# A three-stage float32 kernel on one Trainium2 core: another product order in a phase's last block column, and steps moved to other places of the order

## The chip, the cores and the metric

The program runs on one core of one Trainium2 chip. The metric is the device time of one execution in microseconds (us); the time of a kernel is the median of its runs. A profiled execution gives, beside its own time, the start and the length of every instruction on each engine. PE is TensorE (matmuls), PEld its weight loads, DVE is VectorE, ACT is ScalarE, POOL is GpSimd, and SP is the engine whose queue issues all DMAs of this kernel.

## The reference

Three layers follow one another. B = 2 batches, 768 steps, 8 heads of 64; N = 1536 tokens, 512 features; 8 experts of width 1024; a dense layer of width 2048 whose weights come as 64-bit floats.

```python
def _attn_ref(q, k, v):          # decayed linear attention
    for t in range(S):
        state = gamma * state + einsum('bhd,bhe->bhde', k[:, :, t], v[:, :, t])
        y[:, :, t] = scale * einsum('bhd,bhde->bhe', q[:, :, t], state)

def _moe_ref(x, w_gate, w1, w2):
    logits = x @ w_gate
    P = exp(logits - logits.max())
    for _ in range(8):           # the gate iterations
        P /= P.sum(1, keepdims=True) + 1e-09
        P /= P.sum(0, keepdims=True) + 1e-09
        P *= N / E
    for e in range(E):
        out += P[:, e:e+1] * (maximum(x @ w1[e], 0.0) @ w2[e])

def _moe2_ref(x, w_in, w_out, alpha):
    h = x @ w_in
    g = maximum(h, 0.0) + alpha * minimum(h, 0.0)
    return g @ w_out
```

## The kernel before

After the attention (to 47 us) the kernel runs 20 **phases**, each one a pair of layers for one batch of 768 tokens: phases 0 to 7 are the experts for batch 0, phases 8 to 15 (FAST) the experts for batch 1, phases 16 to 19 the dense layer, cut into two halves of its width for each batch. Every float32 factor is held as two float32r pieces, a high half (a rounded copy, made by ACT) and a low half (the rest, made by DVE or POOL), and `mm3` makes three matmuls of each product of pieces.

**Layer 1** of a phase is computed as a Strassen-like scheme of 7 products for each of 4 block columns j, so 28 products of 6 matmuls. Product p of column j is called (j, p). The list `order` says in which order they stand, and a place in it is a position 0 to 27. What `after` does once a product is issued: (j,1) fills bank A, and ACT copies it to bank B; (j,5) fills D, which is copied to `d` in SBUF (ACT, in dense phases DVE); (j,6) adds to B, and DVE writes E = B + d; (j,7) adds to B again, which must wait until E has been made, and DVE makes B + d a second time (into D, in FAST phases into an SBUF tile `b22`); (j,4) adds to B once more, which must wait for that; (j,3) adds to E and (j,2) to A. `block` then turns a finished bank into the high and low halves of the next layer's input, with later steps of it kept in the list `late` and issued after the next product.

**Layer 2** of the phases outside FAST makes 6 token tiles; each is two half tiles of 12 matmuls over four of the eight blocks of the width ("t0a" uses columns 0 and 1, "t0" columns 2 and 3). These 12 half tiles are positions 28 to 39. FAST phases have a second Strassen-like scheme of 28 units u there, positions 28 to 55.

All other work is put by hand beside this order: `step(ph, pos, fn)` and `at(ph, key, fn)` hang a step behind the product or half tile at that position, and `do` issues the product, what `after` adds, and then the steps in the order in which they were registered. Every engine, SP too, works off its own instructions in the order in which they were issued, and a waiting one holds up those behind it. The steps that matter here:

- `w1_at`: layer 1's weights of column m (n is the phase's first column): four sums (`w1_sum`), then a high and a low half of three parts a, c and b. The low half of b is followed by `w_load(0, m + 2)`, the load of the column after the next into the same one of two buffers; before that buffer can be filled, the store of a part of it to `c1` (in `w1_high`) must have been read out.
- `w2_high`, `w2_low`: high and low halves of layer 2's weights v; the second low half is followed by `w_load(1, n + 2)`.
- `decode_at(ph, bits, power, join, store)`: a 512 KB tile `rd` of 64-bit weights is turned into float32: `bits` (three DVE operations, L702, L704, L707), `power` (ACT, L712), `join` (DVE, L718, L721), `store` (SP) and at once the load of the next tile into the same buffer (L692). A FAST phase decodes two tiles, the first at positions 5, 7, 8 and 10, the second at 19, 21, 23 and 25.
- `gate_max`, `shift`, `rows`, `cols`: the gate. `shift` has one small matmul (`mx`) whose bank DVE clears first (`zeroed`), then operations on DVE and ACT; each `cols` one small matmul (`cs`).
- In FAST phases `t1` to `t4`, `hhigh` and `hlow` (L903) prepare layer 2's input from `b11`, `b12`, `b21` and `b22`.

Of the kernel before, what the change touches and what calls it, by code (L numbers as in the profile page):

```python
# [16 lines left out]
B, H, S, D = 2, 8, 768, 64  # L17
# [28 lines left out]
def tile_kernel(ctx, tc, qkT, kv, ctab, w_gate, w1, w2, w_in, w_out, alpha, out):  # L46
# [254 lines left out]
    with tc.manual_schedule():  # L301
# [491 lines left out]
        def after(ph, n, j, p):  # L793
# [26 lines left out]
            elif p == 7:  # L820
                nc.vector.tensor_tensor(out=banks[n, "D"], in0=banks[n, "B"], in1=banks[n, "d"], op=add)  # L821
                block(ph, n, j, 1, 1, banks[n, "D"])
            elif p == 4:
                block(ph, n, j, 1, 0, banks[n, "B"])
            elif p == 2:
                block(ph, n, j, 0, 0, banks[n, "A"])
            elif p == 3:
                block(ph, n, j, 0, 1, banks[n, "E"])
# [185 lines left out]
        for j in range(1, NJ):  # L1014
            order += [(j, 1), (j, 5), (j - 1, 4), (j, 6), (j - 1, 3), (j, 2), (j, 7)]
        order += [(NJ - 1, 3), (NJ - 1, 4)]
        slots = [f"t{t}{w}" for t in range(TT) for w in ("a", "")]
        todo = []
# [3 lines left out]
        def step(ph, pos, *fns):  # L1022
            if pos >= 60:
                ph, pos = ph + 1, pos - 60
            for fn in fns:
                key = order[pos] if pos < 28 else pos - 28 if ph in FAST else slots[pos - 28]
                at(ph, key, fn)
# [27 lines left out]
        for ph in range(len(PHASES)):  # L1055
# [8 lines left out]
            elif ph < E:  # L1064
                decode_at(ph, 30, 31, 32, 33)
                decode_at(ph, 36, 37, 38, 39)
                prep_at(ph, dve, 9, 19, 9, 21, 23, 24, 27)
# [8 lines left out]
            if fast:  # L1076
# [3 lines left out]
                w1_at(ph, n + 5, pool, dve, 44, 44, 45, 48, 49, 50, 52)  # L1080
            else:
                if ph:
                    w1_at(ph, n + 2, pool, pool, 0, 3, 3, 6, 6, 9, 9)
                else:
                    w1_at(ph, n + 2, pool, pool, 0, 5, 5, 9, 9, 11, 11)
                if ph:
                    w1_at(ph, n + 3, pool, pool, 5, 10, 10, 12, 12, 16, 16)
                else:
                    w1_at(ph, n + 3, pool, pool, 10, 13, 13, 14, 14, 17, 17)
# [3 lines left out]
                early = ((4, 6, 7, dve), (9, 12, 13, dve), (15, 16, 20, dve), (22, 25, 26, dve))  # L1093
                usual = ((12, 12, 12, pool), (17, 17, 17, pool), (19, 19, 19, pool), (23, 23, 23, pool))
                first = ((6, 6, 7, dve), (12, 13, 14, dve), (18, 18, 18, pool), (23, 23, 23, pool))
                for j, (hi, l0, l1, eng) in enumerate(first if ph == 0 else early if ph < E else usual):
                    step(ph, hi, lambda m=n + j: w2_high(m))
                    step(ph, l0, lambda m=n + j, eng=eng: w2_low(m, 0, eng))
                    step(ph, l1, lambda m=n + j, eng=eng: w2_low(m, 1, eng))
# [3 lines left out]
            if fast:  # L1103
                decode_at(ph, 5, 7, 8, 10)
                decode_at(ph, 19, 21, 23, 25)
# [58 lines left out]
        at(0, (3, 4), lambda: sums.update(ps=zeroed("mx", 128)))  # L1164
        at(0, "t0a", shift)
        for it, key in enumerate(("t0", "t1a", "t1", "t2a", "t3a", "t3", "t4a", "t5a")):
            at(0, key, lambda it=it: cols(it))
        for m, keys in ((4, ("t0", "t1a", "t1", "t2a", "t2")), (5, ("t2", "t3a", "t3", "t4", "t4"))):
            at(0, keys[0], *(lambda m=m, q=q: w1_sum(m, q, dve) for q in (0, 1)))
            at(0, keys[1], *(lambda m=m, q=q: w1_sum(m, q, dve) for q in (2, 3)))  # L1170
            for part, key in zip("acb", keys[2:]):
                at(0, key, lambda m=m, part=part: w1_part(m, part, dve))
# [14 lines left out]
        for ph in range(len(PHASES)):  # L1187
# [12 lines left out]
            for t in range(TT):  # L1200
                do(ph, f"t{t}a")
                do(ph, f"t{t}")
# [77 lines left out]
```

## Time and profile before

| | us |
|---|---|
| runs, median (lowest to highest of 3) | 1285.27 (1284.57 to 1286.77) |
| the profiled execution, its time | 1281.88 |
| its span, first to last instruction | 1279.8 |
| PE busy | 1270.3 (99%) |
| DVE, ACT, POOL busy | 956.2 (75%), 639.8 (50%), 427.8 (33%) |
| granted TensorE clock, mean | 1.000 |

The profiled execution lies 3.4 us below the median of the runs, and 2.1 us of its time lie outside its span. Layer 1 of a phase takes some 29.5 us, layer 2 some 32.7 us (29.15 us in FAST phases). Matmuls are pipelined and their shown lengths overlap, so a busy PE still loses time where two starts lie further apart than usual: back to back, matmuls of 384 columns start 0.173 us apart, those of 512 columns 0.226 us.

### The profile page before, as it was taken

The numbers are of one execution on the slowest core, as the hardware profiler recorded it, in microseconds if no ns is written. First come the engines' busy times: TensorE is split into PE (matmuls) and PEld (weight loads), VectorE is DVE, ScalarE is ACT, GpSimd is POOL, SyncE is SP. The second block draws the span as 40 slices with busy tenths as digits, with TensorE's granted clock in tenths as the row PEclk, the third lists the DMA queues.
The fourth block names the chain that finished last, engine by engine and source line by source line (L and its number), as shares of the span: only waits on it lengthen the run. The fifth ranks groups of instructions, "written<-read, shape, count | busy, mean of one in ns | idle before, by whom it ended". The sixth has DMA issues, their size and how long they took to land.

```text
span 1279.8 us, 19739 instructions
## 1 busy us (share of the span) xinstructions
PE 1270.3 (99%) x7276; PEld 1180.6 (92%) x7276; DVE 956.2 (75%) x1551; ACT 639.8 (50%) x1157; POOL 427.8 (33%) x396
## 2 busy tenths in 40 slices
PE   9999999999999999999999999999999999999998
PEld 7888898989898989899999999999999998989897
DVE  6666888888888888868697887878797865686271
ACT  5643544444443435555545464646455473737270
POOL 5743252526161607000031402131304181616160
PEclk9999999999999999999999999999999999999999
DMA  9673898999999999877686858686775862242111
GB/s 357 213 232 120 264 338 277 320 291 312 300 311 291 316 306 306 283 259 239 236 264 217 291 190 289 197 276 206 269 228 190 310 216 83 83 140 93 48 34 50
DMA packets 150671, 295.76 MB, mean 231 GB/s; under 512 B 11904, under 2 KB 75440, under 8 KB 150576
## 3 DMA queue, kind: packets, MB, share of 16 engines
q1 hardware_dynamic: 150576, 294.52, 69.7%
q8 instruction: 57, 0.93, 0.3%
q14 instruction: 38, 0.31, 0.1%
HBM read 197.19 MB, written 97.28 MB: 230 GB/s over the span
## 4 chain that ended last, share of the span: by engine, by line
PE 88%; DVE 5%; ACT 2%; POOL 2%; issue 2%; DMA 1%; POOLq 0%; ACTq 0%
PE o L197 10%; PE o L199 10%; PE o L198 10%; PE B L197 8%; PE B L199 8%; PE B L198 8%; PE A L199 5%; PE A L198 5%; PE A L197 5%; PE D L199 3%; PE D L197 3%; PE D L198 3%; PE E L199 2%; PE E L198 2%; PE E L197 2%
## 5 line engine op out<-in xcount | busy, mean ns | idle before, releaser
L107 POOL TENSOR_TENSOR raw<-raw 128x256 f32<-128x256 f32 x112 | 100.6, 908 | 96.4 <-DMA raw<-wd 28.3
L179 POOL TENSOR_TENSOR pr<-pr 128x256 f32<-128x256 f32 x52 | 49.5, 952 | 205.3 <-DMA pr<-in_w_dram 202.2
L893 ACT ACTIVATE hs<-b 128x768 fp32r<-128x768 f32 x112 | 93.8, 845 | 32.7 <-PE A L199 11.4
L903 DVE TENSOR_TENSOR hs<-b,hs 128x768 fp32r<-128x768 f32 x96 | 92.8, 974 | 12.3 <-ACT hs L893 12.2
L935 POOL TENSOR_TENSOR total<-total,t 128x384 f32<-128x384 f32 x56 | 66.3, 1211 | 103.0 <-DVE t L931 102.7
L805 ACT ACTIVATE B<-A 128x384 f32<-128x384 f32 x80 | 38.7, 484 | 107.8 <-PE A L199 104.6
L808 DVE TENSOR_TENSOR E<-B,d 128x384 f32<-128x384 f32 x80 | 45.0, 562 | 61.7 <-PE B L199 56.8
L261 POOL TENSOR_TENSOR xs<-b,xs 128x384 fp32r<-128x384 f32 x6 | 8.8, 1464 | 197.7 <-ACT xs L257 197.7
L199 PE MATMUL B<-hs,ws 128*128 128x384 f32 x192 | 64.2, 334 | 0.0
L197 PE MATMUL B<-hs,ws 128*128 128x384 f32 x192 | 64.1, 334 | 0.0
L198 PE MATMUL B<-hs,ws 128*128 128x384 f32 x192 | 64.1, 334 | 0.0
L712 ACT ACTIVATE ex<-ex,ebias 128x512 uint32<-128x512 uint32 x32 | 23.0, 720 | 76.7 <-DVE ex L702 76.7
L183 ACT ACTIVATE pw<-pr 128x1024 fp32r<-128x1024 f32 x32 | 33.8, 1057 | 52.8 <-POOL pr L179 29.7
L857 DVE SCALAR_TENSOR_TENSOR total<-o,P,total 128x512 f32<-128x512 f32 x42 | 31.4, 747 | 37.1 <-PE o L199 36.9
L187 DVE TENSOR_TENSOR pr<-pr,pw 128x512 fp32r<-128x512 f32 x64 | 52.0, 843 | 0.0
L179 DVE TENSOR_TENSOR pr<-pr 128x256 f32<-128x256 f32 x76 | 46.9, 617 | 1.7
L851 ACT ACTIVATE total<-o 128x512 f32<-128x512 f32 x18 | 10.8, 598 | 68.1 <-PE o L199 68.1
L197 PE MATMUL A<-hs,ws 128*128 128x384 f32 x128 | 42.9, 335 | 0.0
L198 PE MATMUL A<-hs,ws 128*128 128x384 f32 x128 | 42.8, 335 | 0.0
L199 PE MATMUL A<-hs,ws 128*128 128x384 f32 x128 | 42.8, 334 | 0.0
L821 DVE TENSOR_TENSOR D<-B,d 128x384 f32<-128x384 f32 x48 | 26.8, 558 | 20.2 <-PE B L199 20.2
L800 ACT ACTIVATE d<-D 128x384 f32<-128x384 f32 x64 | 31.2, 488 | 15.9 <-PE D L199 15.8
(3441 smaller groups left out, 4656.8 us busy)
## 6 DMA issues: line engine op xcount, KB each, us to landing
ws<-c SPq DMA_DIRECT2D x112, 512.0 KB, 5.2
raw<-in_w_dram SPq DMA_DIRECT2D x64, 512.0 KB, 4.5
c<-raw SPq DMA_DIRECT2D x32, 512.0 KB, 5.9
pr<-in_w_dram SPq DMA_DIRECT2D x32, 512.0 KB, 5.9
c<-pw SPq DMA_DIRECT2D x32, 512.0 KB, 7.0
c<-pr SPq DMA_DIRECT2D x32, 512.0 KB, 7.2
raw<-c SPq DMA_DIRECT2D x32, 512.0 KB, 5.9
raw<-wd SPq DMA_DIRECT2D x32, 512.0 KB, 3.7
```

What stands on the lines that cost most here:

```text
L107: eng.tensor_tensor(out=out, in0=in0, in1=in1, op=op)
L179: eng.tensor_tensor(out=out, in0=in0, in1=in1, op=op)
L183: nc.scalar.activation(out=ph2[i], in_=pr[i], func=AF.Copy)
L187: nc.vector.tensor_tensor(out=pr[i][:, a].bitcast(F32R), in0=pr[i][:, a], in1=ph2[i][:, a].bitcast(F32), op=ALU.subtract)
L197: nc.tensor.matmul(ps, ah, bh, start=first, stop=False, skip_group_check=True)
L198: nc.tensor.matmul(ps, ah, bl, start=False, stop=False, skip_group_check=True)
L199: nc.tensor.matmul(ps, alo, bh, start=False, stop=last, skip_group_check=True)
L805: nc.scalar.activation(out=banks[n, "B"], in_=banks[n, "A"], func=AF.Copy)
L808: nc.vector.tensor_tensor(out=banks[n, "E"], in0=banks[n, "B"], in1=banks[n, "d"], op=add)
L893: nc.scalar.activation(out=t[:, 0, :], in_=hsource(ph, k), func=func)
L903: nc.vector.tensor_tensor(out=lo, in0=src, in1=hi.bitcast(F32), op=ALU.subtract)
L935: nc.gpsimd.tensor_tensor(out=dst, in0=dst, in1=tt[m, h], op=ALU.add)
```

## The change

It touches only the order in which work is issued and, at some places, the engine that does it.

- In the last column (j = 3) the order (3,1) (3,5) (2,4) (3,6) (2,3) (3,2) (3,7) (3,3) (3,4) becomes (3,1) (3,5) (3,6) (2,4) (2,3) (3,7) (3,2) (3,3) (3,4).
- Outside FAST, `block` of product 7 is no longer issued at once, but after the next product's own step.
- The second decoding of a FAST phase goes from positions 19, 21, 23, 25 to 15, 17, 20, 22.
- Phases 1 to 7: three low halves one position later.
- Dense phases: layer 2 begins with t0a, t1a, t0, t1; the weights v0 and v1 are split at position 1 (phase 16: 8 to 17) and v2's low half at 19.
- Phase 15: the sums of column 65 on DVE at position 42 instead of on POOL at 44.
- Phase 0: low halves of columns 2 and 3 partly on DVE; v1's low halves at 17 and 18 instead of 13 and 14; v2 and v3 at 20 and 24; columns 4 and 5 spread from position 22 on; the clearing of `mx` behind (3,3) and `shift` behind (3,4) instead of (3,4) and t0a, and the eight `cols` from t0a instead of t0.

```diff
--- before.py
+++ after.py
@@ -819,7 +819,7 @@
                     nc.scalar.activation(out=dst, in_=banks[n, key], func=AF.Relu)
             elif p == 7:
                 nc.vector.tensor_tensor(out=banks[n, "D"], in0=banks[n, "B"], in1=banks[n, "d"], op=add)
-                block(ph, n, j, 1, 1, banks[n, "D"])
+                late.append([lambda: block(ph, n, j, 1, 1, banks[n, "D"])])
             elif p == 4:
                 block(ph, n, j, 1, 0, banks[n, "B"])
             elif p == 2:
@@ -1011,10 +1011,17 @@
 
         pool, dve = nc.gpsimd, nc.vector
         order = [(0, 1), (0, 5), (0, 6), (0, 2), (0, 7)]
-        for j in range(1, NJ):
+        for j in range(1, NJ - 1):
             order += [(j, 1), (j, 5), (j - 1, 4), (j, 6), (j - 1, 3), (j, 2), (j, 7)]
+        j = NJ - 1
+        order += [(j, 1), (j, 5), (j, 6), (j - 1, 4), (j - 1, 3), (j, 7), (j, 2)]
         order += [(NJ - 1, 3), (NJ - 1, 4)]
         slots = [f"t{t}{w}" for t in range(TT) for w in ("a", "")]
+        paired = ["t0a", "t1a", "t0", "t1"] + slots[4:]
+
+        def slots_of(ph):
+            return paired if ph >= 2 * E else slots
+
         todo = []
         for ee in range(2):
             todo += [(k, NJ * ee + j, half) for k in range(2) for j in range(NJ) for half in range(2)]
@@ -1023,7 +1030,7 @@
             if pos >= 60:
                 ph, pos = ph + 1, pos - 60
             for fn in fns:
-                key = order[pos] if pos < 28 else pos - 28 if ph in FAST else slots[pos - 28]
+                key = order[pos] if pos < 28 else pos - 28 if ph in FAST else slots_of(ph)[pos - 28]
                 at(ph, key, fn)
 
         def decode_at(ph, *at_):
@@ -1064,7 +1071,7 @@
             elif ph < E:
                 decode_at(ph, 30, 31, 32, 33)
                 decode_at(ph, 36, 37, 38, 39)
-                prep_at(ph, dve, 9, 19, 9, 21, 23, 24, 27)
+                prep_at(ph, dve, 9, 19, 9, 21, 24, 25, 27)
                 prep_at(ph, pool, 25, 25, 25, 29, 30, 30, 31)
                 if ph < 7:
                     prep_at(ph, dve, 31, 31, 31, 33, 34, 34, 35)
@@ -1077,23 +1084,36 @@
                 w1_at(ph, n + 2, pool, dve, 0, 3, 4, 4, 6, 9, 10)
                 w1_at(ph, n + 3, pool, dve, 5, 10, 12, 11, 13, 16, 17)
                 w1_at(ph, n + 4, pool, dve, 36, 36, 38, 39, 40, 42, 43)
-                w1_at(ph, n + 5, pool, dve, 44, 44, 45, 48, 49, 50, 52)
+                if ph < 2 * E - 1:
+                    w1_at(ph, n + 5, pool, dve, 44, 44, 45, 48, 49, 50, 52)
+                else:
+                    w1_at(ph, n + 5, dve, dve, 42, 44, 45, 48, 49, 50, 52)
             else:
                 if ph:
                     w1_at(ph, n + 2, pool, pool, 0, 3, 3, 6, 6, 9, 9)
-                else:
-                    w1_at(ph, n + 2, pool, pool, 0, 5, 5, 9, 9, 11, 11)
-                if ph:
                     w1_at(ph, n + 3, pool, pool, 5, 10, 10, 12, 12, 16, 16)
                 else:
-                    w1_at(ph, n + 3, pool, pool, 10, 13, 13, 14, 14, 17, 17)
+                    step(ph, 0, lambda: w1_adds(2, pool))
+                    step(ph, 10, lambda: w1_adds(3, pool))
+                    for m, part, hi, lo, eng in (
+                        (2, "a", 5, 5, pool), (2, "c", 9, 9, pool), (2, "b", 11, 14, dve),
+                        (3, "a", 13, 16, dve), (3, "c", 14, 14, pool), (3, "b", 17, 17, pool),
+                        (4, "a", 25, 25, dve), (4, "c", 26, 27, dve), (4, "b", 37, 37, dve),
+                        (5, "a", 34, 34, dve), (5, "c", 34, 34, dve), (5, "b", 39, 39, dve),
+                    ):
+                        step(ph, hi, lambda m=m, part=part: w1_high(m, part))
+                        step(ph, lo, lambda m=m, part=part, eng=eng: w1_low(m, part, eng))
+                    for m, q, pos in ((4, 0, 22), (4, 1, 22), (4, 2, 24), (4, 3, 24), *((5, q, 31) for q in range(4))):
+                        step(ph, pos, lambda m=m, q=q: w1_sum(m, q, dve))
                 if ph > 0:
                     w1_at(ph, n + 4, dve, dve, 29, 29, 30, 31, 32, 31, 32)
                     w1_at(ph, n + 5, dve, dve, 33, 33, 34, 35, 36, 35, 36)
-                early = ((4, 6, 7, dve), (9, 12, 13, dve), (15, 16, 20, dve), (22, 25, 26, dve))
-                usual = ((12, 12, 12, pool), (17, 17, 17, pool), (19, 19, 19, pool), (23, 23, 23, pool))
-                first = ((6, 6, 7, dve), (12, 13, 14, dve), (18, 18, 18, pool), (23, 23, 23, pool))
-                for j, (hi, l0, l1, eng) in enumerate(first if ph == 0 else early if ph < E else usual):
+                early = ((4, 6, 7, dve), (9, 12, 13, dve), (15, 16, 21, dve), (22, 25, 26, dve))
+                usual = ((1, 1, 1, pool), (1, 1, 1, pool), (12, 19, 19, pool), (23, 23, 23, pool))
+                turned_in = ((8, 11, 11, pool), (12, 17, 17, pool), (23, 23, 23, pool), (25, 25, 25, pool))
+                first = ((6, 6, 7, dve), (13, 17, 18, dve), (20, 20, 20, pool), (24, 24, 24, pool))
+                kinds = {0: first, 2 * E: turned_in}
+                for j, (hi, l0, l1, eng) in enumerate(kinds.get(ph, early if ph < E else usual)):
                     step(ph, hi, lambda m=n + j: w2_high(m))
                     step(ph, l0, lambda m=n + j, eng=eng: w2_low(m, 0, eng))
                     step(ph, l1, lambda m=n + j, eng=eng: w2_low(m, 1, eng))
@@ -1102,7 +1122,7 @@
                         step(ph, pos, lambda m=n + j: w2_keep(m))
             if fast:
                 decode_at(ph, 5, 7, 8, 10)
-                decode_at(ph, 19, 21, 23, 25)
+                decode_at(ph, 15, 17, 20, 22)
                 if ph > E + 1:
                     for q in range(8):
                         step(ph, (2, 5, 8, 11)[q // 2], lambda m=q // 2, h=q % 2: gather(m, h))
@@ -1161,15 +1181,10 @@
         at(0, (0, 1), lambda: nc.sync.dma_start(out=xd[1][:, :, 4 * C:6 * C], in_=xg[NT // 2 - 1]))
         at(0, (0, 2), lambda: gate_rows(NT // 2 - 1, bank("R"), 3))
         at(0, (0, 7), gate_max)
-        at(0, (3, 4), lambda: sums.update(ps=zeroed("mx", 128)))
-        at(0, "t0a", shift)
-        for it, key in enumerate(("t0", "t1a", "t1", "t2a", "t3a", "t3", "t4a", "t5a")):
+        at(0, (3, 3), lambda: sums.update(ps=zeroed("mx", 128)))
+        at(0, (3, 4), shift)
+        for it, key in enumerate(("t0a", "t0", "t1a", "t2a", "t2", "t3", "t4a", "t5a")):
             at(0, key, lambda it=it: cols(it))
-        for m, keys in ((4, ("t0", "t1a", "t1", "t2a", "t2")), (5, ("t2", "t3a", "t3", "t4", "t4"))):
-            at(0, keys[0], *(lambda m=m, q=q: w1_sum(m, q, dve) for q in (0, 1)))
-            at(0, keys[1], *(lambda m=m, q=q: w1_sum(m, q, dve) for q in (2, 3)))
-            for part, key in zip("acb", keys[2:]):
-                at(0, key, lambda m=m, part=part: w1_part(m, part, dve))
         for t in range(TT):
             at(1, (t // 2 + 1, (6, 2)[t % 2]), lambda t=t: scale0(t))
 
@@ -1197,9 +1212,8 @@
                 for u in range(28):
                     do(ph, u)
                 continue
-            for t in range(TT):
-                do(ph, f"t{t}a")
-                do(ph, f"t{t}")
+            for key in slots_of(ph):
+                do(ph, key)
         held[0].close()
 
 
```

## Rows read from the trace of the kernel before

**Rows 1.** The page, busy time: engine, busy us, share of the span, instructions.

```profile
PE 1270.3 (99%) x7276; PEld 1180.6 (92%) x7276; DVE 956.2 (75%) x1551; ACT 639.8 (50%) x1157; POOL 427.8 (33%) x396
```

**Rows 2.** Waits of PE: engine, what, line, whom for; total us, times, longest us.

```profile
PE B L197 <- DVE b L816: 2.2, 5, 1.1
...
PE B L197 <- ACT B L805: 0.7, 4, 0.2
...
PE D L199 <- POOL wc3l L136: 0.5, 1, 0.5
...
PE cs L671 <- DVE cs L637: 0.4, 1, 0.4
...
PE o L197 <- ACT hh L775: 0.3, 1, 0.3
```

**Rows 3.** PE timeline, phase 9, end of layer 1: start, us, line, instruction.

```profile
637.24 0.33 PE L197 MATMUL A<-xh,wa39h 128*128 128x384 f32 x1
...
640.24 0.34 PE L199 MATMUL E<-xh,wb39l 128*128 128x384 f32 x1
...
640.86 0.44 PE L197 MATMUL B<-xh,wb39h 128*128 128x384 f32 x1 [0.28 <-DVE b L816]
...
641.14 0.34 PE L198 MATMUL B<-xl,wb39h 128*128 128x384 f32 x1
```

**Rows 4.** PE timeline, phase 7, the same place.

```profile
517.06 0.34 PE L199 MATMUL E<-xh,wb31l 128*128 128x384 f32 x1
...
517.35 0.44 PE L197 MATMUL B<-xh,wb31h 128*128 128x384 f32 x1
```

**Rows 5.** Decoding loads: issue (SP timeline), then KB and us to landing; last, all.

```profile
625.97 0.43 SPq L692 DMA_DIRECT2D rd<-in_w_in_dram  x1
...
rd<-in_w_in_dram SPq DMA_DIRECT2D x1, 512.0 KB, 7.0
...
977.76 0.42 SPq L692 DMA_DIRECT2D rd<-in_w_out_dram  x1
...
rd<-in_w_out_dram SPq DMA_DIRECT2D x1, 512.0 KB, 4.9
...
DMA to landing us min/median/max: 3.8/5.9/7.1
```

**Rows 6.** DVE timeline, phase 9.

```profile
629.18 0.57 DVE L808 TENSOR_TENSOR E<-B,d 128x384 f32<-128x384 f32 x1 [1.34 <-PE B L199]
...
631.20 0.69 DVE L136 TENSOR_TENSOR wb39l<-raw,wb39h 128x512 fp32r<-128x512 f32 x1 [1.45 <-ACT wb39h L127]
...
633.15 0.78 DVE L702 TENSOR_SCALAR ex<-rd 128x512 uint32<-128x512 uint32 x1
```

**Rows 7.** DVE timeline, decoding steps in phases 11 and 15.

```profile
755.07 0.68 DVE L718 SCALAR_TENSOR_TENSOR a<-a,ex 128x512 f32<-128x512 f32 x1
...
756.39 0.95 DVE L903 TENSOR_TENSOR hs<-b,hs 128x768 fp32r<-128x768 f32 x1
...
985.71 0.41 DVE L702 TENSOR_SCALAR ex<-rd 128x512 uint32<-128x512 uint32 x1
...
987.10 0.95 DVE L903 TENSOR_TENSOR hs<-b,hs 128x768 fp32r<-128x768 f32 x1
```

**Rows 8.** Phase 0: SP timeline, then us to landing of a store and a load.

```profile
68.65 0.42 SPq L118 DMA_DIRECT2D c<-raw  x1
...
c<-raw SPq DMA_DIRECT2D x1, 512.0 KB, 5.2
...
73.94 0.33 SPq L92 DMA_DIRECT2D raw<-in_w_dram  x1
...
raw<-in_w_dram SPq DMA_DIRECT2D x1, 512.0 KB, 5.9
```

**Rows 9.** Dense phase 17: DVE timeline, then PE timeline.

```profile
1107.81 0.61 DVE L774 SCALAR_TENSOR_TENSOR A<-A,sg,n 128x384 f32<-128x384 f32 x1
...
1109.13 0.33 PE L197 MATMUL B<-xh,wb70h 128*128 128x384 f32 x1
```

## Prediction

> **What bounds the kernel now.** First the busy times: PE works in 99% of the span [rows 1]. PE's matmuls are the same before and after, so only time in which PE waits can be won, and new waits can be added. Second, the waits of PE, which name the late partner [rows 2]. They show only idle time over 0.15 us, so, third, the starts in the PE timeline: in phase 9 the last product starts 0.62 us after the matmul before it instead of 0.173, and the next matmul 0.28 us after that instead of 0.173 [rows 3]. The wait thus costs 0.55 us where the list of waits says 0.28, because a stopped PE loses 0.1 us more at its restart. I count that way. In phases 1 to 7 the same place has a short wait that the list leaves out: 0.29 us between two starts [rows 4] and 0.1 us at the restart, so 0.22 us. Over the whole trace such excesses come to about 14 us; that is all that any reordering could win. The fourth view is that of the loads and of the engines that wait for them, since the change moves steps closer to their loads.
>
> **What is won, place by place.** (1) Last product, (3,4). It waits for DVE's second B + d after (3,7); before, one product lay between them, now two (2.08 us). In FAST phases 9, 10, 12 and 13 this is worth 0.55 us each, in phase 15 1.33 us (the longest wait of DVE b in rows 2, and the way of counting of rows 3): 3.5 us. In phases 2 to 7 it is 0.22 us each [rows 4] and in phase 1 0.5 us: 1.8 us. (2) In phases 1 to 7 (2,7) starts 0.03 us late and restarts 0.1 us late, behind DVE's E, which queues behind a low half that waits for a `block` of product 7. That `block` now comes a product later and DVE runs the other half of v1 first: 0.9 us over seven phases. (3) Phase 0: wa3 and wc3 come from POOL too late [rows 2]; wa3 goes to DVE, wc3 no longer queues behind it: 1.3 us. One gate iteration is late for its `cs` matmul [rows 2], 0.7 us with the restart. (4) Dense phases: t0 needs the halves of (3,4), which go through four steps on ACT and DVE; with t1a in between they have 5.4 us instead of 2.7, and (3,4) two products of cover: 0.85, 0.6, 0.75 and 0.1 us in phases 16 to 19 (ACT hh in [rows 2]), 2.3 us. Sum of the gains: 3.5 + 1.8 + 0.9 + 1.3 + 0.7 + 2.3 = 10.5 us.
>
> **What stays.** In the dense phases (3,6) waits 0.44 us for ACT's copy B (ACT B L805, four times, in [rows 2]). That copy comes earlier now, as v1's high half and the `block` of (2,7) no longer stand before it. But (3,6) comes one product earlier too, and before the copy stands the high half of A, which needs DVE's L774, started at 1107.81 and 0.61 long; then 0.46 for that half and 0.58 to the copy's end give 1109.5, against 1109.13 at which position 21 could start [rows 9]. About 0.4 us remain plus a restart: I count 0; bounds -0.5 and +1.8 us for all four.
>
> **What is added in FAST phases: DVE and ACT wait for `rd`.** The second tile is loaded behind the first `store` at position 10, which doesn't move. In phase 9 the load is issued at 625.97 and lands 7.0 us later, in phase 15 at 977.76 and 4.9 us later [rows 5]; of these eight loads the others take 5.4 to 7.1 us. At position 15 DVE is done with E at about 629.7 [rows 6], so `bits` stands at the head of its queue 3.2 us before its data. Behind it wait on DVE: wb's low half, t1, `b22` of (2,7), `join`, hlow, and E of (3,6). On ACT, `power` at 17 waits for `bits`, and behind it the x copy and the copy B for (3,6). Before, `bits` came at 633.15, 0.2 us after the landing, and cost nothing.
> Followed to the product that then ends last, (3,7), which must wait for E: `bits` 1.39 us and `join` 1.32 us [rows 7], wb, t1 and `b22` together 1.95 us [rows 6], hlow 0.9 us (its length less overlap, [rows 7]), E 0.57 us: about 6.15 us from landing to PE. Position 24 starts at 637.24 in phase 9 [rows 3], 4.3 us after the landing; the eight leads, phases 8 to 15, are 4.4, 4.3, 5.8, 5.3, 4.2, 5.8, 5.7 and 6.8 us. So PE loses 1.8, 1.8, 0.3, 0.8, 2.0, 0.4, 0.5 and 0 us, together 7.6, and seven restarts of 0.1: 8.3 us. Waits of (3,6) and (2,4) before it lie inside this. Bounds: 0, if every load took the shortest 3.8 us, and some 16 us if all took 7.1 [rows 5]. I take the rows of the same eight loads, since nothing ahead of them in SP's queue changes.
> A rule speaks against this price. The Trainium skill, DMA: Bandwidth & Descriptors, section "Anatomy of one DMA", gives a transfer as 2.0 us plus its bytes over 436 GB/s. For 512 KB that is an estimate of 3.2 us, by which `rd` would be there when DVE asks and the 8.3 us would be 0. The rows say 4.9 to 7.0 us [rows 5], on queues that carry other transfers, and I go by them.
>
> **What is added in phase 0.** Before, the load of v3 was queued ahead of that of column 5; now its trigger is at 18, behind the latter's at 17. That one waits until c1 of column 3 has been read out: before, the store issued at 68.65 took 5.2 us and the load went out at 73.94, just behind it [rows 8]. Now the store can go at 67.0 (POOL's sums end there), so column 5 loads from 72.2 and v3 from 72.7; with 5.1 to 5.9 us [rows 8] v3 is there at about 77.8. Its high half stands at 24 on ACT, before the halves of (3,2), (3,7), wa4, (3,3), wc4 and (3,4). From landing to the cleared `mx` bank: high half 0.95, two relus 0.8, wa4's high half 0.5 on ACT, its low half 0.6, two low halves 0.95, the clearing 0.2 on DVE, handoffs 0.2: 4.2 us, so PE's `mx` matmul starts at 82.0. Without the old 1.3 us of waits (3,4) ends at 78.1: 3.9 us of wait. After it, DVE has a low half and wc4's (1.35 us) ahead of `shift`, and the first `cs` stands after one half tile instead of a place in which nothing was late: 0.9 us. With two restarts 5.0 us. Bounds: 2.1 us if v3 lands at 75.1 as before, 6.5 us if at 79.4.
>
> **Small.** In phases 17 to 19 four low halves of v0 and v1 now stand on POOL before wa, the sums and wc of column 2; wc is ready within 0.2 us of its use: 0.45 us (0 to 1.0). The copy for (3,6) costs 0.2 us more by its restarts. Column 65's sums on DVE in phase 15: the last hlow comes level with its unit, 0.3 us (0 to 1). Column 6 and 7 load later in phase 0, and POOL has 1 us of slack left in phase 1: 0. The gathers, the steps one position later and the unchanged tail after t5: 0, hidden by PE's matmuls.
>
> **Sum.** -10.5 + 8.3 + 5.0 + 0.95 = +3.75 us. On the profiled execution 1281.88 becomes 1285.6; the median of the runs lies 3.4 us higher, so 1289.0.
>
> **Rivals.** *Faster:* the loads come in time. The price of `rd` falls to 0 once the second load lands within 5.1 us of its issue (637.24 - 6.15 - 625.97); the shortest of all such loads takes 3.8 us [rows 5]. Then FAST phases keep their 3.5 us, phase 0 loses 2.1, and -10.5 + 2.1 + 0.95 = -7.5 gives 1277.8. For it: only 1 to 2 us have to be missing. Against it: the eight loads of before, of which one alone is that quick. By the rule of the Trainium skill named above it is also the time to expect. Chance 0.2. *No change:* one of the two waits bites half. v3's load isn't held up by column 5's, or `rd` lands a microsecond sooner where it is latest: costs of 10 to 11 us, 1285 to 1286. Chance 0.25. *Slower (the forecast)*, with its upper bounds for phase 0 and POOL: 1288 to 1294. Chance 0.55. *The half tiles do nothing*, because t1a itself waits for a bank or a half: 2.3 us less gain, 1291.3, inside the forecast's range.
> The likeliest case alone has 1287.9 to 1294; the range of all is 1279.5 to 1294.0, leaving out the lower half of the faster case and the highest bound of `rd`. A measurement of this kernel tells about 0.2%, 2.6 us, from no change.
>
> **What would show it.** Right: in FAST phases DVE L702 begins at the landing of `rd`, about 20.7 us after the start of phases 9 and 12 and 19.2 us in 10 and 13, with an idle time before it put down to that DMA, and PE waits at (3,6), (2,4) or (3,7); in phase 0 PE waits some 4 us for `mx`, ACT before v3's high half; no wait of PE for `b` at (3,4), and none for hh in layer 2 of the dense phases. Wrong: L702 without idle time before it, PE with no waits between positions 21 and 24, or v3's high half before 76 us. If the waits are there and the time is still lower, the gains were undercounted.

## The result: 1.4% slower, 17.2 us where 3.75 were forecast

The changed kernel takes 1302.16 us (median of 4 runs, 1301.66 to 1304.81), the kernel before 1284.92 in the same runs: ratio 1.014, 95% interval 1.0117 to 1.0163. The forecast was 1289.0 with a range to 1294.0. The sign was right, the size wrong: +17.2 us instead of +3.75. The profiled executions compare as 1299.47 against 1279.83 us of span, +19.6.

First the page's busy times of the changed kernel, which answer to [rows 1]: PE is busy for 4 us more, from 99% to 98% of a longer span, and the other engines work as before.

```profile
PE 1274.3 (98%) x7276; PEld 1182.3 (91%) x7276; DVE 960.3 (74%) x1557; ACT 643.7 (50%) x1157; POOL 422.2 (32%) x390
```

Second the waits of PE in the changed kernel (engine, what, line, whom for; us, times, longest), to be set beside [rows 2]:

```profile
PE B L197 <- ACT B L805: 5.2, 6, 1.0
PE mx L649 <- DVE mx L637: 4.5, 1, 4.5
PE B L197 <- DVE b L816: 4.5, 7, 1.0
PE B L197 <- DVE E L808: 3.9, 8, 0.7
PE B L197 <- DVE D L821: 2.3, 7, 0.3
```

The waits of (3,4), for wa3 and wc3, for `cs` and for hh are gone, as forecast. Five groups of new ones stand in their place. Where they lie is read from the starts of PE's products. This table sums, for every stage, how much longer it took than before in the two profiled executions, with the forecast's own terms beside it (the dense stage ends with its last matmul):

| stage | forecast, us | measured, us |
|---|---|---|
| phase 0 | -1.3 - 0.7 + 5.0 = +3.0 | +4.17 |
| layer 1 of phases 1 to 7 | -1.8 - 0.9 = -2.7 | +1.76 |
| layer 1 of phases 8 to 15 | -3.5 + 8.3 = +4.8 | +10.86 |
| dense phases 16 to 19, both layers | -2.3 + 0.65 = -1.65 | +2.87 |
| rest (start, end, phase 15's sums) | +0.3 | -0.02 |
| sum | +3.75 | +19.64 |

Of the 15.9 us between the two sums, 6.1 lie in the FAST phases, 4.5 in the dense phases, 4.5 in phases 1 to 7 and 1.2 in phase 0.

### The profile page after: what moved, and what is told of

Same layout as the page of the kernel before. It is cut to its first block, busy times and chain, and to the rows that moved or that the text cites. A ratio compares the mean times of both kernels' runs of the same rounds, so it can differ in the third digit from the quotient of the medians.

```text
span 1299.5 us, 19748 instructions
## 1 busy us (share of the span) xinstructions
PE 1274.3 (98%) x7276; PEld 1182.3 (91%) x7276; DVE 960.3 (74%) x1557; ACT 643.7 (50%) x1157; POOL 422.2 (32%) x390
## 4 chain that ended last, share of the span: by engine, by line
PE 83%; DVE 8%; DMA 4%; ACT 3%; issue 2%; SPq 1%; POOL 0%; ACTq 0%; DVEq 0%; POOLq 0%
PE o L197 10%; PE o L199 10%; PE o L198 10%; PE B L197 7%; PE B L198 7%; PE B L199 7%; PE A L199 5%; PE A L197 5%; PE A L198 5%; PE E L199 2%; PE E L198 2%; PE E L197 2%; PE D L197 2%; PE D L199 2%; PE D L198 2%
## 5 line engine op out<-in xcount | busy, mean ns | idle before, releaser
L107 POOL TENSOR_TENSOR raw<-raw 128x256 f32<-128x256 f32 x108 | 96.1, 900 | 111.4 <-DMA raw<-in_w_dram 39.5
L893 ACT ACTIVATE hs<-b 128x768 fp32r<-128x768 f32 x112 | 93.8, 845 | 51.9 <-DVE b L873 19.6
L179 POOL TENSOR_TENSOR pr<-pr 128x256 f32<-128x256 f32 x52 | 46.8, 899 | 202.7 <-DMA pr<-in_w_dram 199.6
L808 DVE TENSOR_TENSOR E<-B,d 128x384 f32<-128x384 f32 x80 | 45.0, 562 | 48.9 <-PE B L199 40.5
L179 DVE TENSOR_TENSOR pr<-pr 128x256 f32<-128x256 f32 x76 | 54.6, 718 | 1.7
L821 DVE TENSOR_TENSOR D<-B,d 128x384 f32<-128x384 f32 x48 | 26.9, 560 | 27.8 <-PE B L199 27.8
```

The lines of the kernel that those rows point to most:

```text
L107: eng.tensor_tensor(out=out, in0=in0, in1=in1, op=op)
L179: eng.tensor_tensor(out=out, in0=in0, in1=in1, op=op)
L808: nc.vector.tensor_tensor(out=banks[n, "E"], in0=banks[n, "B"], in1=banks[n, "d"], op=add)
L893: nc.scalar.activation(out=t[:, 0, :], in_=hsource(ph, k), func=func)
```

## Where the time went: three readings of the changed trace

**FAST phases.** The DVE timeline of phase 9 (start, length, line, instruction, idle time before it and its cause), then POOL's and PE's:

```profile
640.29 0.43 DVE L702 TENSOR_SCALAR ex<-rd 128x512 uint32<-128x512 uint32 x1 [3.16 <-DMA rd<-in_w_in_dram]
...
642.30 1.78 DVE L873 TENSOR_TENSOR b<-b,b 128x768 f32<-128x768 f32 x1
644.01 0.55 DVE L816 TENSOR_TENSOR b<-B,d 128x384 f32<-128x384 f32 x1
644.48 1.02 DVE L718 SCALAR_TENSOR_TENSOR a<-a,ex 128x512 f32<-128x512 f32 x1
...
647.01 0.56 DVE L808 TENSOR_TENSOR E<-B,d 128x384 f32<-128x384 f32 x1
```

```profile
641.98 1.29 POOL L261 TENSOR_TENSOR xs<-b,xs 128x384 fp32r<-128x384 f32 x1 [122.39 <-ACT xs L257]
643.23 1.71 POOL L253 TENSOR_TENSOR ta<-b 128x384 f32<-128x384 f32 x1
```

```profile
642.33 0.44 PE L197 MATMUL B<-xh,wc39h 128*128 128x384 f32 x1 [0.66 <-ACT B L805]
...
644.61 0.44 PE L197 MATMUL B<-xh,wb38h 128*128 128x384 f32 x1 [0.97 <-DVE b L816]
...
647.62 0.45 PE L197 MATMUL B<-xh,wc39h 128*128 128x384 f32 x1 [0.66 <-DVE E L808]
```

`bits` (L702) starts at the landing of `rd`, 20.68 us after the phase's start (the forecast said about 20.7), and PE waits at (3,6), (2,4) and (3,7). But from the landing to (3,7) the chain takes 7.35 us, not 6.15. Two steps are longer than the rows of before had them: t1 (L873) with 1.78 us instead of 0.95, and L718 with 1.02 instead of 0.68. Both ran beside a POOL instruction: t1 starts at 642.30, POOL's low half ends at 643.27, and t1 ends 0.82 us later, nearly its whole length. So DVE was not slow: as these times read, it stood still until POOL had finished, inside an instruction that the profile shows as busy. POOL's next one, `ta`, began while t1 ran and took 1.71 us; the same one took 1.20 in the kernel before.

**Phases 1 to 7.** A wait at a place where there was none, position 14, (1,4). DVE, POOL and PE in phase 2:

```profile
193.38 3.27 DVE L179 TENSOR_TENSOR pr<-pr 128x256 f32<-128x256 f32 x2
...
197.03 0.55 DVE L821 TENSOR_TENSOR D<-B,d 128x384 f32<-128x384 f32 x1
```

```profile
193.07 1.85 POOL L136 TENSOR_TENSOR wc10l<-raw,wc10h 128x768 fp32r<-128x768 f32 x1
194.88 1.48 POOL L136 TENSOR_TENSOR wb10l<-raw,wb10h 128x512 fp32r<-128x512 f32 x1
```

```profile
196.95 0.34 PE L199 MATMUL D<-xh,wc10l 128*128 128x384 f32 x1
197.64 0.44 PE L197 MATMUL B<-xh,wb9h 128*128 128x384 f32 x1 [0.35 <-DVE D L821]
```

The two prep sums (L179) take 3.27 us. Alone such a sum takes 0.43 (the median of the 76, before and after). They begin 0.3 us after POOL's low half of wc; the first ends 0.28 us after that half (195.20 and 194.92), the second 0.28 us after the next (196.64 and 196.36). In the kernel before the first sum began 0.13 us ahead of the same POOL instruction and got through, so that the pair took 2.45:

```profile
188.65 2.45 DVE L179 TENSOR_TENSOR pr<-pr 128x256 f32<-128x256 f32 x2
```

```profile
188.78 2.04 POOL L136 TENSOR_TENSOR wc10l<-raw,wc10h 128x768 fp32r<-128x768 f32 x1
```

The low half from the `block` of (0,7), issued a product later, came 0.8 us later on DVE, in front of v0's halves; it used up DVE's idle time there and moved it by 0.23 us at this place. POOL's low half in turn began 0.21 us earlier in the phase than before. Together they put the sum behind POOL's start.

Over the whole trace of before the rule has no exception in these rows: the 48 sums that began with POOL idle took 0.41 to 0.43 us, the 28 others 0.45 to 1.96. Each of these 28, and each of the 28 in the changed kernel, ended 0.28 to 0.29 us after the POOL instruction that ran when it began. DVE instructions with an operand in PSUM (L764, L808, L821) took the same 0.54 to 0.57 either way. The Trainium skill, SBUF — State Buffer, section "Who interferes with whom", agrees: a DVE instruction with two SBUF inputs contends with a GpSimd instruction that reads SBUF, the port pair that they share is an exclusive lock, issue order decides who blocks, and a DVE instruction with at most one SBUF input does not contend outside the modes that use both of DVE's ports. The forecast took durations from single rows and didn't ask what POOL did beside them.

**Phase 0.** ACT, then PE, then the windows (us, busy time of each engine with its instructions, granted clock, DMA share, GB/s):

```profile
77.70 1.06 ACT L146 ACTIVATE v3h<-raw 128x1024 fp32r<-128x1024 f32 x1 [2.80 <-DMA raw<-in_w_dram]
```

```profile
83.05 0.80 PE L649 MATMUL mx<-dm,ones 128*128 128x128 f32 x2 [4.52 <-DVE mx L637]
```

```profile
83.40:86.00 2.60, 2.60 (x8) 2.12 (x8) 2.02 (x8) 0.37 (x1) 0.00 (x0) 0.50 0.83 321
86.00:88.00 2.00, 2.00 (x10) 1.65 (x10) 1.10 (x5) 0.00 (x0) 0.00 (x0) 0.95 1.05 369
```

This is the forecast's chain: v3 lands at 77.68 (forecast 77.8), ACT stands before its high half, and PE's `mx` matmul is 4.7 us late instead of 3.9. Of the rest, most fits POOL again: wa4's low half on DVE took 1.81 us instead of 0.68, beside POOL's halves of v3. What the forecast hadn't priced at all: behind the wait TensorE's granted clock is 0.50, the lower of its two levels (1.2 GHz), and the next six matmuls cost 1.35 us more. Five more versions below keep this phase 0 as it is; in their traces it is 4.6 to 5.9 us longer than before, so the 4.17 of the table is the lowest of six.

## Experiments

**Taking the parts back, one at a time.** Four versions of the changed kernel.

```diff
-                decode_at(ph, 15, 17, 20, 22)
+                decode_at(ph, 19, 21, 23, 25)
```

> The changed kernel with the second decoding of a FAST phase back at positions 19, 21, 23, 25. Theory (the wait for rd): all the new waits of PE at positions 21, 22 and 24 of phases 8 to 15, 14.4 us with their restarts, come from the decoding that stands ahead of its data; then DVE's L702 starts without idle time in phases 9 to 15, layer 1 of these phases takes 29.15 to 29.3 us each, and the time is 1302.2 - 14.4 = 1287.8, 1287 to 1289. Rival (the product order): (3,6) and (3,7) one product earlier are late by themselves, whatever the decoding; then PE still waits at positions 21 or 24, a third or more of the 14.4 us stays and the time is 1292 or more.

Ratio to before 1.0051 (1.0034 to 1.0067), 1288.25 us. Layer 1 of phases 8 to 15 fell by 13.9 us, to 29.2 to 29.6 us each in phases 9 to 15, and PE has no wait over 0.15 us left there. So the decoding, at these places, is the whole of it, and the new order is worth 3.0 us in these phases (forecast 3.5).

```diff
-                first = ((6, 6, 7, dve), (13, 17, 18, dve), (20, 20, 20, pool), (24, 24, 24, pool))
+                first = ((6, 6, 7, dve), (12, 13, 14, dve), (20, 20, 20, pool), (24, 24, 24, pool))
```

> The changed kernel with v1 in phase 0 split at 12, 13 and 14 instead of 13, 17 and 18, so that the load of v3 is triggered before that of column 5. Theory (queue order): v3's load goes out some 5 us sooner, its high half no longer holds up ACT at position 24, the 4.7 us of PE at the mx matmul fall to under 1 us, and the clock doesn't fall to 0.50 behind it (1.35 us): 5 us less, 1297. Rival (too much work): ACT and DVE simply have too many steps between positions 20 and 28 of phase 0, the wait at mx stays at 2.5 us or more, and the time is 1299.5 or more.

1300.57 us, ratio 1.0144 (1.0129 to 1.0159): no gain that the time shows, since phase 8 was 1.2 us longer in this trace (other landings of `rd`). Phase 0 alone is read from the trace: 69.69 us instead of 72.47. PE's waits in phase 0:

```profile
PE mx L649 <- DVE mx L637: 2.2, 1, 2.2
PE cs L671 <- DVE cs L637: 0.4, 1, 0.4
```

v3 landed at 73.79 and ACT no longer waits for it, the clock stays up, but half of the wait is left. There DVE's two sums for column 4 took 2.55 us beside POOL's halves of v3, where two alone take 0.85. Taking back the load's place in SP's queue takes 2.3 us of the wait and the 1.35 of the clock away; the other 2.3 us stay, nearly what the rival had. But the two halves can't be given to one theory each. The third version below leaves the load where it is (v3's high half begins 30.4 us after the phase's start, as in the changed kernel), and its wait at `mx` is 2.5 us too; the fourth, which has both edits, still waits 2.4. Some 0.9 us came back at wa3 and `cs`.

```diff
-                late.append([lambda: block(ph, n, j, 1, 1, banks[n, "D"])])
+                block(ph, n, j, 1, 1, banks[n, "D"])
```

> The changed kernel with block of product 7 issued at once again. Theory (the late block makes both new waits): in phases 1 to 7 the 0.6 us at (1,4) go and 0.13 us at (2,7) come back, together -3.3 us; in the dense phases the wait at (3,6) falls from 1.16 to the 0.44 us of before and those at (2,7) go, together -3.2 us; 1295.7, 1295 to 1297. Rival (the new order makes them): both waits stay, under 1.5 us are gained, 1301 or more.

1297.35 us, ratio 1.0119 (1.0104 to 1.0135). In the dense phases layer 1 fell by 4.0 us (3.2 expected), and phase 0 by 2.6, which neither theory had. In phases 1 to 7 the wait at (1,4) went, but a longer one came, at (3,6) for ACT's copy B, so that these phases are 2.0 us longer:

```profile
PE B L197 <- ACT B L805: 3.6, 7, 0.6
```

ACT's copy of (3,1) then queues behind the half of (2,7)'s `block`, and that waits for DVE. So the late `block` is needed behind (2,7) in phases 1 to 7, costs there by what it moves in the earlier columns, and costs in the dense phases as a whole; the columns were not undone one by one.

> The three edits together: decoding back, v1 early in phase 0, block of product 7 at once. If the three causes are apart from one another and the only costs, the gains add up: 1302.2 - 14.4 - 5 - 6.5 = 1276, under both kernels, with the covers of the new order, of phase 0 and of the half tiles left over. If they overlap, or if the gains of the prediction (10.5 us) aren't there, it ends at 1280 or more.

1283.84 us, ratio 1.001 (1.000 to 1.0021): 17 us of span back, but no gain over before. The wait of the third version at (3,6) comes with it (phases 1 to 7 are 3.6 us longer than before), and phase 0 stays 2.6 us longer, with a new wait of PE for wa3 (0.8 us).

**Is it POOL that makes DVE's steps longer?** Three versions of the changed kernel.

```diff
-                    for keys in ((12, 17, 18, 27), (37, 39, 41, 45), (46, 48, 50, 55)):
+                    for keys in ((12, 26, 27, 29), (37, 39, 41, 45), (46, 48, 50, 55)):
```

> The changed kernel with the high and low half and the store of the first x copy of phases 9 to 14 at 26, 27 and 29 instead of 17, 18 and 27. Theory (DVE shut out by POOL): t1 on DVE (L873) no longer begins beside POOL's low half, takes 0.95 us again instead of 1.78, and PE's waits at (2,4) and (3,7) are shorter by 0.8 us in each of these six phases: -5 us, and one step less on ACT before the copy B for (3,6), 0.4 us in phases 9 and 12. Rival: the chain from the landing of rd to PE is as long without POOL; under 2 us gained.

1296.18 us, ratio 1.0108 (1.0094 to 1.0122). The same chain, in phase 10 of the changed kernel and then of this one:

```profile
700.37 0.43 DVE L702 TENSOR_SCALAR ex<-rd 128x512 uint32<-128x512 uint32 x1 [1.79 <-DMA rd<-in_w_in_dram]
...
702.37 1.78 DVE L873 TENSOR_TENSOR b<-b,b 128x768 f32<-128x768 f32 x1
...
707.08 0.56 DVE L808 TENSOR_TENSOR E<-B,d 128x384 f32<-128x384 f32 x1
```

```profile
700.78 0.43 DVE L702 TENSOR_SCALAR ex<-rd 128x512 uint32<-128x512 uint32 x1 [1.84 <-DMA rd<-in_w_in_dram]
...
702.79 0.95 DVE L873 TENSOR_TENSOR b<-b,b 128x768 f32<-128x768 f32 x1
...
706.32 0.56 DVE L808 TENSOR_TENSOR E<-B,d 128x384 f32<-128x384 f32 x1
```

From L702 to E 5.54 us instead of 6.71. In all six phases the chain from the landing to the end of E now takes 6.1 us, the forecast's sum; in the changed kernel it takes 7.0 or 7.3 there, and 6.1 in phase 8, which has no x copy. Layer 1 of phases 9 to 14 is 5.8 us shorter in all, close to the 5.6 us by which the forecast had priced the decoding too low (13.9 against 8.3); what is left of the decoding's cost is 7.5 us (layer 1 of phases 8 to 15 takes 243.0 us, against 235.5 with the decoding back). A part of the 5.8 belongs to ACT, which has one step less before the copy for (3,6) in phases 9 and 12 (0.3 us each).

```diff
-                prep_at(ph, dve, 9, 19, 9, 21, 24, 25, 27)
+                prep_at(ph, dve, 16, 19, 9, 21, 24, 25, 27)
```

> The changed kernel with the first two prep sums of phases 1 to 7 (DVE L179, both inputs in SBUF) at position 16 instead of 9. Theory (DVE shut out by POOL): the wait at (1,4) comes from these two sums, which begin while POOL's wc low half runs and take 3.3 us instead of the 0.85 us that they take alone; moved away, the 0.6 us at (1,4) go in seven phases, -4.2 us against the changed kernel, if nothing new is late at 16 (rest: -3 to -4.5). Rival (the late block alone): DVE's B + d for (1,7) is late because its queue is longer by the late steps, whoever runs on POOL; then half of the wait or more stays at (1,4), under 2 us gained.

The wait at (1,4) is gone in all seven phases, but 0.44 of its 0.60 us came back at (3,7) in phases 2 to 7, where E now stands behind the moved sums, and all of it at (3,6) in phase 1. Layer 1 of phases 1 to 7 is 1.25 us shorter; the time is the same as the changed kernel's, 1301.09 us, ratio 1.0142 (1.0127 to 1.0158). Moving the sums also shortens the queue before (1,4), so this doesn't part the two theories. The next one does: it leaves the sums where they are and puts an instruction on POOL that reads nothing.

```diff
-        eng.tensor_tensor(out=lo, in0=src, in1=hi.bitcast(F32), op=ALU.subtract)
+        if part in "cb" and 2 * NJ <= n - 2 < E * NJ and n % NJ == 2:
+            eng.memset(lo.bitcast(F32), 0.0)
+        else:
+            eng.tensor_tensor(out=lo, in0=src, in1=hi.bitcast(F32), op=ALU.subtract)
```

> The changed kernel, in which POOL's low halves of parts c and b of the third column in phases 2 to 7 are left out and a memset of the same tile, which reads nothing, stands in their place (the low halves are zero, a smaller product). Theory (DVE shut out by a POOL instruction that reads SBUF): DVE's two prep sums at position 9 take 0.85 us together instead of 3.3, and the wait at (1,4) goes: layer 1 of phases 2 to 7 falls from 29.8 to 29.2 us each. Rival (the queue is too long by itself): the sums may be shorter, but the wait at (1,4) stays above 0.3 us.

DVE and POOL in phase 2 (the line numbers are 3 higher here):

```profile
196.16 0.87 DVE L182 TENSOR_TENSOR pr<-pr 128x256 f32<-128x256 f32 x2
...
198.07 0.57 DVE L824 TENSOR_TENSOR D<-B,d 128x384 f32<-128x384 f32 x1 [0.57 <-PE B L202]
```

```profile
195.84 0.74 POOL L137 MEMSET wc10l<- 128x768 f32 x1
196.52 0.53 POOL L137 MEMSET wb10l<- 128x512 f32 x1
```

Two runs, 1295.88 and 1300.31 us, ratio 1.0117 (1.009 to 1.0144); the reading is that of the phases. The sums run beside POOL's writes in 0.87 us, DVE then waits for PE and not the other way round, and layer 1 of phases 2 to 7 takes 29.13 to 29.30 us instead of 29.80. Phase 1, where POOL still reads, keeps its wait. This settles it for phases 2 to 7, where the edit stands. The memsets are shorter than what they replace, 0.74 us against 1.85, but they overlapped both sums and didn't stop them.

**Is it the data or the place of the decoding?**

```diff
-                decode_at(ph, 5, 7, 8, 10)
+                decode_at(ph, 2, 4, 5, 7)
```

> The changed kernel with the first decoding of a FAST phase at 2, 4, 5 and 7 instead of 5, 7, 8 and 10, so that the second tile's load is issued 3.1 us sooner, and the second decoding left at 15, 17, 20, 22. Theory (the wait for rd): it lands 4.9 to 7 us after its issue, now before position 15 or at most 0.5 us after it; the waits of PE at 21, 22 and 24 fall from 14.4 us to under 3 us: -11 to -14 us, some 1289. Rival (the positions): the decoding's six DVE and ACT steps are too much between 15 and 22 wherever the data is; half of the 14.4 us or more stays, 1295 or more.

1291.62 us, ratio 1.0075 (1.0061 to 1.0089). The second tile's load goes out 5.1 us sooner in phases 9 to 14 (8.65 us after the phase's start instead of 13.75). Three products make 3.1 us of that; the rest is SP's queue, on which the store now stands ahead of the loads that wait for the low half of wb, and no longer behind them. So the decoding at 15 to 22 costs nothing: in phases 9 to 15 the second `bits` has no idle time before it, and layer 1 takes 29.2 us. Only phase 8 lost 3.3 us. Its first `bits` now stands ahead of its data, which landed at 567.94, and after that it waited 2 us more for the store of a transposed tile `tt` (to `xd`), from whose pool of buffers `ex` comes too:

```profile
570.00 0.43 DVE L702 TENSOR_SCALAR ex<-rd 128x512 uint32<-128x512 uint32 x1 [4.10 <-DMA xd<-tt]
```

The eight second loads took 4.2 to 5.0 us now instead of 4.9 to 7.2. The landing times of both loads of a phase, from the second of phase 9 to the second of phase 15, of the changed kernel and then of this one (us from issue to landing):

```profile
DMA to landing us min/median/max: 4.4/5.2/7.2
```

```profile
DMA to landing us min/median/max: 4.2/4.7/5.0
```

```diff
-                decode_at(ph, 19, 21, 23, 25)
+                decode_at(ph, 15, 17, 20, 22)
```

This one edit in the kernel before:

> The kernel before, with the second decoding at 15, 17, 20, 22 as the only edit. Theory (the wait for rd): the old product order doesn't protect from it; PE waits at (2,4), then at position 21, until DVE has come from the landing to B + d of (2,7), some 4 us: 10 to 16 us more than before, 1.008 to 1.0125. Rival: the moves need each other to hurt; with (3,6) and (3,7) one product later the decoding costs under 4 us, ratio under 1.003.

1297.71 us, ratio 1.0116 (1.0094 to 1.0138): layer 1 of the FAST phases is 15.0 us longer. PE's waits in these phases stand at one place, (2,4):

```profile
PE B L197 <- DVE b L816: 13.2, 8, 2.9
```

The decoding needs no other part of the change to hurt. In phases 9 and 12 the clock fell too; the windows of phase 9:

```profile
637.00:639.50 2.50, 0.50 (x3) 0.18 (x2) 2.50 (x4) 0.66 (x2) 2.50 (x2) 1.00 0.50 107
639.50:643.00 3.50, 3.42 (x11) 3.42 (x12) 3.43 (x5) 1.31 (x3) 0.42 (x1) 0.51 0.77 271
```

**What is worth keeping.** A version with the new order and the half tiles, the second decoding at 19 to 25, phase 0 and column 65 as before, the late `block` only behind (2,7) of phases 0 to 7 (a FAST phase has no `block` there), v0 and v1 of phases 17 to 19 split early.

```diff
+                if ph < 2 * E and j == NJ - 2:
+                    late.append([lambda: block(ph, n, j, 1, 1, banks[n, "D"])])
+                else:
+                    block(ph, n, j, 1, 1, banks[n, "D"])
...
+                usual = ((1, 1, 1, pool), (1, 1, 7, pool), (12, 19, 19, pool), (23, 23, 23, pool))
+                turned_in = ((12, 12, 12, pool), (17, 17, 17, pool), (19, 19, 19, pool), (23, 23, 23, pool))
```

> A version that keeps the product order and the half tiles and drops what cost time: the second decoding at 19 to 25, phase 0 and column 65 as before, block of product 7 late only behind (2,7) of phases 1 to 15, and in the dense phases v0 and v1 split early except in phase 16. By the phases of the runs so far: FAST -3.0, phases 1 to 7 -0.3 us each (-2.1), layer 2 of the dense phases -1.7, their layer 1 -0.5 to +1, phase 0 nothing: -6 to -7.3 us against the kernel before, a ratio of 0.9945 to 0.9955. If the covers only work with the rest of the change, it is within 0.2% of before.

1274.96 us, ratio 0.9945 (0.9933 to 0.9958). Phases 1 to 7 have gained 1.7 us in layer 1, the FAST phases 3.3, layer 2 of the dense phases 1.7, phase 0 0.8. The dense phases' layer 1 is 0.5 us longer: it waits at (3,6), which stands one product earlier than before. The next version gives the dense phases the old order back.

```diff
+        plain = order[:19] + [(j, 1), (j, 5), (j - 1, 4), (j, 6), (j - 1, 3), (j, 2), (j, 7), (j, 3), (j, 4)]
+
+        def order_of(ph):
+            return plain if ph >= 2 * E else order
...
-                    w1_at(ph, n + 3, pool, pool, 10, 13, 13, 14, 14, 17, 17)
+                    for part, hi, lo, low in (("a", 13, 15, dve), ("c", 14, 14, pool), ("b", 17, 17, pool)):
```

> The version before this one (product order in phases 0 to 15, half tiles, decoding at 19 to 25) with the old product order in the dense phases and wa3's low half on DVE in phase 0. Theory: in the dense phases ACT's copy B is done at a fixed time, so that (3,6) one product later has 1.04 us more: the waits at (3,6), 0.53 us in phases 17 to 19 and 1.48 us in 16, go or fall to 0.44, -2.6 us; the 0.36 us for wa3 go and the 0.73 us for wc3 shrink, -0.4 to -1. Against the kernel before 0.9915 to 0.9925. Rival: in the old order with half tiles (3,4) or t0 becomes late instead and takes it back; 0.9945 or more.

1272.66 us, ratio 0.9919 (0.9904 to 0.9933), the fastest of all. Layer 1 of phases 17 to 19 takes 29.12 us, without a wait; 16 keeps 0.44. These are PE's only waits over 0.15 us between 20 and 1290 us:

```profile
PE D L199 <- POOL wc3l L136: 0.4, 1, 0.4
PE B L197 <- ACT B L805: 0.2, 1, 0.2
```

Last, the half tiles by themselves, taken out of the version with 0.9945.

```diff
-        paired = ["t0a", "t1a", "t0", "t1"] + slots[4:]
+        paired = slots
```

> The first of these versions (ratio 0.9945) with the half tiles of layer 2 in their old order. Theory: t0 then waits for the halves of (3,4) again, in layer 2 of phases 16 to 19 as before the change: +0.8, +0.3, +0.5, +0.1, together 1.7 us, ratio 0.9958. Rival: the new product order has moved the last products' halves enough that t0 isn't late: no difference.

1275.52 us, ratio 0.9941 (0.9926 to 0.9956), no difference that the time shows. In the traces layer 2 of phase 16 is 0.9 us longer without them, that of phases 17 to 19 the same. So of the 1.7 us that layer 2 of the dense phases gained, 0.9 in phase 16 belong to the half tiles; in 17 to 19 the rest of the version does as well without them. Whether that is the product order or the weights split early, no run parts.

## The prediction, step by step

- **Gains, 10.5 us.** Mostly right. (3,4) has no wait left; FAST gave 3.0 to 3.3 us of 3.5. For phases 1 to 7 the waits at (3,4) and (2,7) are gone in the changed kernel, hidden by the new one; once the late `block` stood only behind (2,7), the 1.8 us of (3,4) were left (1.7 measured) and the wait at (2,7), the 0.9, was back. wa3 and wc3 came in time. Layer 2 of the dense phases gave 1.7 of 2.3, though not by the half tiles alone.
- **`rd`, 8.3 us: right cause, wrong size.** Landing, waiting engine and the three places of PE's waits were as forecast, the price 13.9. The step that failed is the sum of the chain, 6.15 us: its durations were rows without POOL beside them. (Of the 1.95 us for wb, t1 and `b22` the rows that it names show only wb's 0.69.) As a sum it holds where POOL is idle, 6.1 us; with POOL's low half and `ta` beside t1 and L718 it was 7.0 to 7.3, and as the lead was already used up all of it went to PE in six phases. The upper bound of 16 us had been put on the landing time alone and then left out of the range.
- **Dense (3,6), 0 with bounds -0.5 and +1.8: wrong.** It cost 2.9 us. The step that failed is "v1's high half and the `block` of (2,7) no longer stand before it". They don't, but the `block`s of (0,7) and (1,7) are later too, and behind (1,7) ACT's half now waits behind v2's high half; DVE's E for (2,6) waits for that, and everything after it, up to ACT's copy B. Phase 17 of the changed kernel, ACT, DVE and PE:

```profile
1121.93 1.09 ACT L146 ACTIVATE v70h<-raw 128x1024 fp32r<-128x1024 f32 x1
1122.88 0.61 ACT L775 ACTIVATE hh<-D,sg 128x384 fp32r<-128x384 f32 x1
...
1128.44 0.48 ACT L805 ACTIVATE B<-A 128x384 f32<-128x384 f32 x1
```

```profile
1123.52 0.62 DVE L777 SCALAR_TENSOR_TENSOR hl<-D,sg,hh 128x384 fp32r<-128x384 f32 x1 [1.41 <-ACT hh L775]
1124.05 0.56 DVE L808 TENSOR_TENSOR E<-B,d 128x384 f32<-128x384 f32 x1
```

```profile
1128.97 0.44 PE L197 MATMUL B<-xh,wc71h 128*128 128x384 f32 x1 [0.89 <-ACT B L805]
```

In the third version, with the `block` at once, 0.3 of the 2.9 us are left, and layer 1 is 4.0 us shorter: the late `block` had also cost 1.2 us at (2,7). The 0.45 us for wc of column 2 came out as 1.0.
- **Phases 1 to 7: a missing term.** The late `block` was counted as a gain at (2,7), and nowhere was it asked what else its steps displace. A shift of 0.23 us on DVE and 0.21 on POOL cost 0.6 us in each phase, because it changed who began first, DVE's sum or POOL's low half.
- **Phase 0, 5.0 us: nearly right.** 4.7 us at `mx`, and nothing at `cs`, where 0.9 had been expected; instead 1.35 us of clock. The step that fell short is the queue order as the one cause of the wait: without it half of the wait stays, and without the late `block` half of it goes with the queue order as it is.
- **The transfer rule.** The second loads of the FAST phases took 4.9 to 7.2 us, so the choice to go by the rows was right. The estimate of 3.2 us that the prediction worked out from the Trainium skill, DMA: Bandwidth & Descriptors, section "Anatomy of one DMA", was under the quickest of all decoding loads (4.0 us in this trace). That section gives its fit for transfers issued through GpSimd, as its heading says; these are issued on SP's queue.
- **Rivals.** The faster one needed second loads within 5.1 us; 7 of the 8 were later, and the chain was longer as well.

## What to carry over

A step that is moved takes its length from what runs beside it at the new place. Where VectorE's steps read two SBUF operands, look at GpSimd's row of the same microseconds before adding up a chain; such a wait hides inside the busy time. When a part of an edit is applied to every column or phase, price it at each place where it acts, not only at the one for which it looks meant, and put an edit's load ahead of the edit: the same decoding cost 14 us or, in seven of eight phases, nothing, by 5 us of earlier issue.

## Not expected of the hardware

- A VectorE sum with two SBUF operands that began while GpSimd read SBUF took up to 1.96 us instead of 0.43. The end was the same each time: all 56 such sums of the two traces ended 0.28 to 0.29 us after GpSimd's instruction. Beside GpSimd writing alone (the memsets) the 12 sums took their normal 0.41 to 0.43 us.
- The granted clock fell to 0.50 after PE had waited 4.7 us in phase 0, and in other runs after 2.2 and 3.1 us (the decoding alone, phases 9 and 12) and 2.6 us (the early load, phase 8); after waits of 2.3 to 2.5 us in phase 0 of three versions it did not fall. In the six versions with the same phase 0 the wait was 4.7 to 5.5 us, and between 6 and 12 matmuls behind it ran at the lower level, each 0.2 us longer: the same stretch of code then took 72.5 to 74.2 us.
